# A decode kernel's last stage: FFN down projection and output projection in two column tiles, finer weight pieces, two stores

## The chip, the cores and the metric

The kernel runs on one core of one Trainium2 chip. The metric is the device time of one execution in microseconds (us). A profile belongs to one execution; its "span" runs from the first to the last recorded instruction and is about 1.7 us shorter than the device time. The profile also records the clock granted to PE as a share of full speed; in these traces it is 1.00 or 0.50 ("half clock"). The unchanged kernel took 201.09 us (median of 3 executions, 200.91 to 204.61).

The engines are called PE (TensorE matmul), PEld (its weight load), DVE (VectorE), ACT (ScalarE) and SP (SyncE). SPq and ACTq are DMA issues by the sequencers of SP and ACT.

## The reference

Four decode tokens of width 512 go through grouped-query attention over a window of 4096 cached positions (32 query heads, 8 key/value heads of width 128) and, from the same `x`, through a gated ReLU FFN of width 1792. A scalar gate mixes the two. Cut to what matters here:

```python
g = sigmoid((x * gate_w).sum(-1, keepdims=True))          # [4, 1, 1]
o = softmax(q @ k.T * Dh**-0.5) @ v                       # q = x @ wq; 4096 keys
a = o.reshape(4, 1, 4096) @ wo                            # output projection, wo: [4096, 512]
h = relu(x @ W_gate) * (x @ W_up)                         # [4, 1, 1792]
b = h @ W_down                                            # down projection, W_down: [1792, 512]
return g * a + (1 - g) * b                                # [4, 1, 512]
```

Keys, values and weights are 81 MB of bf16, and each is read once. This stream of loads is nearly the whole time.

## The kernel before

SP issues all loads in one fixed order. The last are W_down ("wd") and wo in five pieces of 16, 8, 4, 2 and 2 of its 32 blocks (a block is 128 rows by 512 columns, 128 KB):

```python
WO_PIECES = ((0, 16), (16, 24), (24, 28), (28, 30), (30, 32))
# ... in the order of loads:
return o + [("wg",), ("wu",), ("v", NSET - 1), ("wd",)] + [("wo", p) for p in range(len(WO_PIECES))]
```

Down projection and output projection accumulate into the same four rows of one PSUM bank, `ACC`, one after the other. The down projection's result is scaled by `1 - g` into SBUF (`T2`) before the output projection may overwrite the bank, and `FIN` combines both:

```python
def FFN():
    for i in range(14):
        mm(banks[ACC][0:4, :], hT[:, 4 * i:4 * i + 4], Wd[:, 512 * i:512 * i + 512], i == 0, i == 13, ...)
def WO(p):
    lo, hi = WO_PIECES[p]
    w = [("WO", p), ("T2",)] + [("E", "OQ", s) for s in range(NSET)]     # the piece, T2, attention's result
    for i in range(lo, hi):
        mm(banks[ACC][0:4, :], oq[:, i, :], Wo[:, i, :], i == 0, i == 31, ...)
# VectorE
def T2():   # t2 = (1 - g) * ACC
    v.tensor_scalar(t2[:, :], banks[ACC][0:4, :], gg[:, 1:2], None, op0=ALU.mult)
def FIN():  # osum = g * ACC + t2
    v.scalar_tensor_tensor(osum[:, :], banks[ACC][0:4, :], gg[:, 0:1], t2[:, :], ALU.mult, ALU.add)
# SyncE, at the end of its queue
e.dma_start(out.rearrange("b o d -> (b o) d"), osum[0:4, :])
```

(Cuts: waits and events of FFN, T2 and FIN.)

## Time and profile before

| | before |
|---|---|
| time, median | 201.09 us |
| span of the profiled execution | 199.34 us |
| loads' share of the 16 DMA engines' span | 95.2% |
| last piece of wo has landed | 194.73 us |
| PE has finished the output projection | 196.88 us |

First, two lines of the page: the queue of loads (packets, MB, share of 16 engines' span), and the engines' shares of the chain that ended last (the work followed back from the last instruction, at each step to what it had waited for).

```profile
q1 hardware_dynamic: 3760, 81.01, 95.2%
DMA 73%; PE 21%; DVE 2%; SPq 2%; issue 0%
```

The loads take the DMA engines nearly the whole span. The chain's end, in order of time (start us, duration us, what):

```profile
149.34 40.41 DMA slots<-in_A_wo_dram
189.75 0.04 issue
189.80 7.08 PE bank L317 x32
196.88 0.02 issue
196.90 0.74 DVE osum L583
```

And the timeline of that stage (start us, duration us, engine, line, operation, tiles, count, and in brackets how long the engine was idle before and what ended that):

```profile
185.14 3.18 PE L317 MATMUL bank<-wdsb,hT 128*4 128x512 bf16 x14
188.36 0.74 DVE L579 TENSOR_SCALAR t<-bank,gg 4x512 f32<-4x512 f32 x1 [2.88 <-PE bank L317]
189.80 7.07 PE L317 MATMUL bank<-slots,oq 128*4 128x512 bf16 x32 [1.48 <-DMA slots<-in_A_wo_dram]
196.90 0.74 DVE L583 SCALAR_TENSOR_TENSOR osum<-bank,gg,t 4x512 bf16<-4x512 f32 x1 [7.81 <-PE bank L317]
197.67 0.29 SPq L276 DMA_DIRECT2D out_dram<-osum  x1
```

The projection begins when the first piece, half of wo, has landed. From there it runs without a pause at 221 ns per matmul. The trace also records when each of the 16 DMA engines reports its part of a transfer; the last report of the five pieces came at 189.75, 192.25, 193.46, 194.10 and 194.73. So PE finished 2.15 us after the last weight had landed, and at the very end the kernel is limited by PE, not by DMA.

### The profile page before, as it was taken

Reading aid. Unit: us, or ns where it says so; the run is one execution under the profiler, and the core shown is the slowest. Engines: PE = TensorE matmul, PEld = TensorE weight load, DVE = VectorE, ACT = ScalarE, POOL = GpSimd, SP = SyncE. Lnnn points to the kernel's source line nnn. Section 1 sums busy time; section 2 is a strip of 40 time slices with the busy share of each in tenths; the row PEclk is TensorE's granted clock in tenths of the full one; section 3 lists DMA queues with packets and bytes.
Section 4 is the critical chain, followed back from the end, with each engine's and each line's share of the span. In section 5 each row is a group of like instructions: output and inputs, shape, how many; then the busy total and the mean of one; then the engine's idle time right before and its main releaser. Section 6 shows DMA issues by size and latency. Waiting matters only on the chain.

```text
span 199.3 us, 4082 instructions
## 1 busy us (share of the span) xinstructions
PE 145.7 (73%) x1806; PEld 110.9 (56%) x1806; DVE 104.7 (53%) x244; ACT 67.6 (34%) x70; POOL 13.2 (7%) x38
## 2 busy tenths in 40 slices
PE   0039865997199839974998599639974997577795
PEld 0039522875197639754976587439754975434231
DVE  2017566886068637862596388607862786310201
ACT  2006522751435343524353455134524451410000
POOL 7774000000000000000000000000000000000000
PEclk9999999999579996997699789988998799576999
DMA  5999999999999999999999999999999999999960
GB/s 210 434 415 427 429 444 434 454 419 427 418 427 434 437 427 431 421 441 437 427 427 424 436 424 421 431 422 434 450 434 418 415 411 448 432 408 424 401 253 1
DMA packets 3778, 81.28 MB, mean 408 GB/s; under 512 B 552, under 2 KB 560, under 8 KB 944
## 3 DMA queue, kind: packets, MB, share of 16 engines
q1 hardware_dynamic: 3760, 81.01, 95.2%
q8 instruction: 14, 0.23, 0.5%
q14 instruction: 4, 0.03, 0.0%
HBM read 81.01 MB, written 0.00 MB: 406 GB/s over the span
## 4 chain that ended last, share of the span: by engine, by line
DMA 73%; PE 21%; DVE 2%; SPq 2%; issue 0%
DMA slots<-in_A_k_cache_dram 43%; DMA slots<-in_A_wo_dram 20%; DMA slots<-in_A_wq_dram 11%; PE bank L321 10%; PE bank L317 10%; SPq L250 2%; DVE qblk L525 1%; DVE osum L583 0%; DVE sc L535 0%; DVE pe L510 0%; DVE pe L512 0%; DVE gp L515 0%
## 5 line engine op out<-in xcount | busy, mean ns | idle before, releaser
L321 PE MATMUL bank<-identf,slots 128*128 128x128 f32 x512 | 73.2, 304 | 31.4 <-DMA slots<-in_A_k_cache_dram 31.4
L321 PEld LDWEIGHTS bank<-identf,slots 128*128 128x128 f32 x512 | 65.5, 159 | 39.3 <-DMA slots<-in_A_k_cache_dram 32.1
L503 DVE COPY slots<-bank 128x1024 bf16<-128x1024 bf16 x80 | 54.3, 690 | 51.0 <-PE bank L321 49.4
L596 ACT ACTIVATE slots<-bank 128x1024 bf16<-128x1024 bf16 x48 | 47.8, 1022 | 63.6 <-PE bank L321 63.4
L618 ACT ACTIVATE pe<-sc,negmax 128x2048 bf16<-128x2048 bf16 x8 | 16.0, 2001 | 37.9 <-DVE negmax L547 37.9
L535 DVE TENSOR_SCALAR_CACHE_REDUCE sc<-bank 128x512 bf16<-128x512 f32 x32 | 22.1, 692 | 3.6 <-PE bank L317 1.2
L317 PE MATMUL bank<-slots,qblk 128*32 128x512 bf16 x256 | 20.5, 394 | 1.3 <-DVE qblk L525 1.2
L317 PE MATMUL bank<-slots,pT 128*32 128x256 bf16 x512 | 17.0, 290 | 1.7 <-DMA slots<-in_A_v_cache_dram 1.7
L317 PEld LDWEIGHTS bank<-slots,pT 128*32 128x32 bf16 x512 | 14.5, 102 | 4.2 <-DMA slots<-in_A_v_cache_dram 1.7
L321 PE MATMUL bank<-identb,pe 128*128 128x128 bf16 x128 | 11.6, 261 | 2.2 <-ACT pe L618 2.2
L553 DVE COPY pT<-bank 128x1024 bf16<-128x1024 bf16 x16 | 10.6, 686 | 3.9 <-PE bank L321 3.8
L317 PE MATMUL bank<-maskr,maskl 128*32 128x512 bf16 x128 | 12.5, 378 | 0.0
L321 PEld LDWEIGHTS bank<-identb,pe 128*128 128x128 bf16 x128 | 10.8, 123 | 2.8 <-ACT pe L618 2.3
L561 DVE TENSOR_SCALAR osb<-bank,recip 128x256 bf16<-128x256 f32 x8 | 3.9, 483 | 12.9 <-PE bank L317 12.9
L317 PE MATMUL bank<-rd,grpb 128*128 128x8 bf16 x8 | 1.4, 179 | 10.1 <-DVE rd L541 10.1
L317 PEld LDWEIGHTS bank<-rd,grpb 128*128 128x128 bf16 x8 | 0.8, 95 | 14.1 <-DVE rd L541 14.1
L317 PE MATMUL bank<-slots,oq 128*4 128x512 bf16 x32 | 7.1, 379 | 1.5 <-DMA slots<-in_A_wo_dram 1.5
L317 PEld LDWEIGHTS bank<-slots,qblk 128*32 128x32 bf16 x256 | 4.6, 95 | 6.1 <-issue 3.5
L317 PEld LDWEIGHTS bank<-slots,oq 128*4 128x4 bf16 x32 | 2.6, 85 | 5.9 <-DMA slots<-in_A_wo_dram 2.0
L317 PEld LDWEIGHTS bank<-maskr,maskl 128*32 128x32 bf16 x128 | 3.4, 95 | 3.9
L317 PE MATMUL bank<-slots,xT 128*4 128x512 bf16 (+1 forms) x64 | 5.1, 476 | 0.3 <-DMA slots<-in_A_wq_dram 0.3
L583 DVE SCALAR_TENSOR_TENSOR osum<-bank,gg,t 4x512 bf16<-4x512 f32 x1 | 0.7, 739 | 7.8 <-PE bank L317 7.8
(57 smaller groups left out, 58.9 us busy)
## 6 DMA issues: line engine op xcount, KB each, us to landing
slots<-in_A_k_cache_dram SPq DMA_DIRECT2D x8, 4096.0 KB, 42.7
slots<-in_A_v_cache_dram SPq DMA_DIRECT2D x8, 4096.0 KB, 33.5
slots<-in_A_wq_dram SPq DMA_DIRECT2D x1, 4096.0 KB, 21.1
slots<-in_A_wo_dram SPq DMA_DIRECT2D x1, 2048.0 KB, 40.4
slots<-in_B_W_gate_dram SPq DMA_DIRECT2D x1, 1792.0 KB, 38.5
slots<-in_B_W_up_dram SPq DMA_DIRECT2D x1, 1792.0 KB, 42.1
wdsb<-in_B_W_down_dram SPq DMA_DIRECT2D x1, 1792.0 KB, 36.1
slots<-in_A_wo_dram SPq DMA_DIRECT2D x1, 1024.0 KB, 42.4
```

Source lines behind the costliest of these rows:

```text
L250: E.op(lambda: e.dma_start(dst, src), ev=ev, waits=waits, ctr=ctr)
L317: E.op(lambda: t.matmul(out_, lhsT, rhs, start=start, stop=stop, tile_position=pos, skip_group_check=True), ev=ev, waits=waits)
L321: E.op(lambda: t.transpose(out_, in_, idn), ev=ev, waits=waits)
L503: E.op(lambda: v.tensor_copy(kt_dst(s, g), bankb[tr(key)]), ev=("E",) + key, waits=[key])
L525: E.op(lambda dst=dst, r=r, b=b: v.tensor_copy(dst, src[r, :, :, :, b]), ev=("E",) + key if (u, b) == (1, 3) else None, waits=[key, ("QZ",)])
L535: E.op(lambda: v.tensor_scalar(sc[:, 512 * f:512 * f + 512], banks[scb(key)], 1.0, None, op0=ALU.mult, op1=ALU.max, accum_out=mx4[:, f:f + ...
L553: E.op(lambda: v.tensor_copy(dst, bankb[tr(key)]), ev=("E",) + key, waits=[key] + ([("PV", s - 2)] if s >= 2 else []))
L561: E.op(lambda: v.tensor_scalar(osb[:, s % 2, :], ob(s), recip[:, s % 2:s % 2 + 1], None, op0=ALU.mult), ev=("NORM", s), waits=[("E", "RS", ...
L583: E.op(lambda: v.scalar_tensor_tensor(osum[:, :], banks[ACC][0:4, :], gg[:, 0:1], t2[:, :], ALU.mult, ALU.add), ev=("OSUM",), waits=[("WOP ...
L596: E.op(lambda: a.activation(kt_dst(s, g), bankb[tr(key)], ACTF.Copy), ev=("E",) + key, waits=[key])
L618: E.op(lambda: a.activation(pe[:, :], sc[:, :], ACTF.Exp, bias=negmax[:, s % 2:s % 2 + 1], scale=SCALE, accum_out=rowsum[:, s % 2:s % 2 + ...
```

## The change

The intent is to have less to do after the last weight has landed. The two projections write 256 columns each to PSUM rows 0 to 3 and 64 to 67, by matmuls at array columns 0 and 64. T2 and FIN then work on 128 rows by 256 columns (only eight rows carry results; the bank is cleared at the start, so that the others hold defined values). The result lies on two groups of rows and needs two stores, one from SP and one from ACT. The first piece of wo is halved, and a 64-byte load, "again", is put last in the queue. The diff's core:

```diff
-WO_PIECES = ((0, 16), (16, 24), (24, 28), (28, 30), (30, 32))
+WO_PIECES = ((0, 8), (8, 16), (16, 24), (24, 28), (28, 30), (30, 32))
+OUTT = 2
+OW = 512 // OUTT
+OR = 128 // OUTT
@@ order of loads
-    ... + [("wo", p) for p in range(len(WO_PIECES))]
+    ... + [("wo", p) for p in range(len(WO_PIECES))] + [("again",)]
@@ FFN (WO and the gate's Z likewise)
-                mm(banks[ACC][0:4, :], hT[:, 4 * i:4 * i + 4], Wd[:, 512 * i:512 * i + 512], i == 0, i == 13, ...)
+                for j in range(OUTT):
+                    x = 512 * i + OW * j
+                    mm(banks[ACC][OR * j:OR * j + 4, 0:OW], hT[:, 4 * i:4 * i + 4], Wd[:, x:x + OW], i == 0, i == 13,
+                       ..., pos=(0, OR * j))
@@ FIN (T2 likewise)
-            v.scalar_tensor_tensor(osum[:, :], banks[ACC][0:4, :], gg[:, 0:1], t2[:, :], ALU.mult, ALU.add)
+            v.scalar_tensor_tensor(osum[:, :], banks[ACC][:, 0:OW], gg[:, 0:1], t2[:, :], ALU.mult, ALU.add)
@@ stores: t = 0 from SP, t = 1 from ACT
-        e.dma_start(out.rearrange("b o d -> (b o) d"), osum[0:4, :])
+        e.dma_start(out.rearrange("b o d -> (b o) d")[:, OW * t:OW * t + OW], osum[OR * t:OR * t + 4, :])
```

More of the change, by code (lines that the diff above doesn't have):

```diff
@@ L109, in _alloc @@
     sb("gwT", [128, 4], BF16)
+    sb("again", [8, 4], BF16)
     sb("osb", [128, 2, 256], BF16)
@@ L127, in _alloc @@
     sb("recip", [128, 2], FP32)
-    sb("ge", [4, 2], FP32)
-    sb("gp", [4, 2], FP32)
-    sb("gg", [4, 2], FP32)
-    sb("t2", [4, 512], FP32)
-    sb("osum", [4, 512], BF16)
+    sb("ge", [128, 2], FP32)
+    sb("gp", [128, 2], FP32)
+    sb("gg", [128, 2], FP32)
+    sb("t2", [128, OW], FP32)
+    sb("osum", [128, OW], BF16)
     R["banks"] = [ctx.enter_context(nc.psum_tensor(f"bank{i}", [128, 512], FP32)) for i in range(8)]
@@ L154, in _dma_order @@
         o += [("k", s), ("v", s - 1)]
-    return o + [("wg",), ("wu",), ("v", NSET - 1), ("wd",)] + [("wo", p) for p in range(len(WO_PIECES))]
+    return o + [("wg",), ("wu",), ("v", NSET - 1), ("wd",)] + [("wo", p) for p in range(len(WO_PIECES))] + [("again",)]
 def _slots():
@@ L164, in _slots @@
         k = it[0]
-        if k in ("x", "gw", "wd") or (k == "wo" and it[1] > 0):
+        if k in ("x", "gw", "wd", "again") or (k == "wo" and it[1] > 0):
             continue
@@ L244, in ob, with store @@
         return banks[OB][:, 256 * (s % 2):256 * (s % 2) + 256]
+    def store(E, e, t):
+        E.op(lambda: e.dma_start(out.rearrange("b o d -> (b o) d")[:, OW * t:OW * t + OW], osum[OR * t:OR * t + 4, :]),
+             ev=("OUT", t), waits=[("OSUM",)], ctr=f"d_out{t}")
     def sync(e):
@@ L258, in sync @@
                 load(("GW",), "d_gw", gwT[:, :], gate_w.rearrange("(p t) -> p t", t=4))
+            elif k == "again":
+                load(("AGAIN",), "d_again", R["again"][0:8, :], gate_w[0:32].rearrange("(p t) -> p t", t=4))
             elif k == "wq":
@@ L275, in sync @@
                      waits=w)
-        E.op(lambda: e.dma_start(out.rearrange("b o d -> (b o) d"), osum[0:4, :]), ev=("OUT",), waits=[("OSUM",)],
-             ctr="d_out")
-        E.wait([("OUT",)])
+        for t in range(0, OUTT, 2):
+            store(E, e, t)
+        E.wait([("OUT", t) for t in range(OUTT)] + [("AGAIN",)])
     def gpsimd(e):
@@ L340, in Z @@
             for q in range(4):
-                mm(banks[ACC][0:4, 0:1], xT[:, 4 * q:4 * q + 4], gwT[:, q:q + 1], q == 0, q == 3,
-                   ev=("Z",) if q == 3 else None, waits=[("E", "XT"), ("GW",)])
+                for j in range(OUTT):
+                    mm(banks[ACC][OR * j:OR * j + 4, 0:1], xT[:, 4 * q:4 * q + 4], gwT[:, q:q + 1], q == 0, q == 3,
+                       ev=("Z",) if (q, j) == (3, OUTT - 1) else None, waits=[("E", "XT"), ("GW",), ("INIT",)],
+                       pos=(0, OR * j))
         def Q():
@@ L436, in FFN @@
             for i in range(14):
-                mm(banks[ACC][0:4, :], hT[:, 4 * i:4 * i + 4], Wd[:, 512 * i:512 * i + 512], i == 0, i == 13,
-                   ev=("FFN",) if i == 13 else None, waits=[("E", "HT"), ("WD",), ("GE",)])
+                for j in range(OUTT):
+                    x = 512 * i + OW * j
+                    mm(banks[ACC][OR * j:OR * j + 4, 0:OW], hT[:, 4 * i:4 * i + 4], Wd[:, x:x + OW], i == 0, i == 13,
+                       ev=("FFN",) if (i, j) == (13, OUTT - 1) else None, waits=[("E", "HT"), ("WD",), ("GE",)],
+                       pos=(0, OR * j))
         def WO(p):
@@ L443, in WO @@
             for i in range(lo, hi):
-                mm(banks[ACC][0:4, :], oq[:, i, :], Wo[:, i, :], i == 0, i == 31, ev=("WOP", p) if i == hi - 1 else None,
-                   waits=w if i == lo else ())
+                for j in range(OUTT):
+                    mm(banks[ACC][OR * j:OR * j + 4, 0:OW], oq[:, i, :], Wo[:, i, OW * j:OW * j + OW], i == 0, i == 31,
+                       ev=("WOP", p) if (i, j) == (hi - 1, OUTT - 1) else None, waits=w if (i, j) == (lo, 0) else (),
+                       pos=(0, OR * j))
         fns = dict(KT=KT, XT=XT, Z=Z, Q=Q, QT=QT, SC=SC, PT=PT, PV=PV, SW=SW, RS=RS, OQ=OQ, WO=WO, GU=GU, HT=HT, FFN=FFN)
@@ L497, in INIT @@
             E.op(lambda: v.memset(qblk[:, :, :, :], 0.0), ev=("QZ",))
-            for bk in SCB:
-                E.op(lambda bk=bk: v.memset(banks[bk], 0.0), ev=("INIT",) if bk == SCB[-1] else None)
+            for bk in SCB + (ACC,):
+                E.op(lambda bk=bk: v.memset(banks[bk], 0.0), ev=("INIT",) if bk == ACC else None)
         def EKT(s, g):
@@ L578, in T2 @@
         def T2():
-            E.op(lambda: v.tensor_scalar(t2[:, :], banks[ACC][0:4, :], gg[:, 1:2], None, op0=ALU.mult), ev=("T2",),
+            E.op(lambda: v.tensor_scalar(t2[:, :], banks[ACC][:, 0:OW], gg[:, 1:2], None, op0=ALU.mult), ev=("T2",),
                  waits=[("FFN",), ("G",)])
         def FIN():
-            E.op(lambda: v.scalar_tensor_tensor(osum[:, :], banks[ACC][0:4, :], gg[:, 0:1], t2[:, :], ALU.mult, ALU.add),
+            E.op(lambda: v.scalar_tensor_tensor(osum[:, :], banks[ACC][:, 0:OW], gg[:, 0:1], t2[:, :], ALU.mult, ALU.add),
                  ev=("OSUM",), waits=[("WOP", len(WO_PIECES) - 1), ("T2",), ("G",)])
@@ L606, in GE @@
             for u in range(2):
-                E.op(lambda u=u: a.activation(ge[:, u:u + 1], banks[ACC][0:4, 0:1], ACTF.Exp, scale=-1.0 if u == 0 else 1.0),
+                E.op(lambda u=u: a.activation(ge[:, u:u + 1], banks[ACC][:, 0:1], ACTF.Exp, scale=-1.0 if u == 0 else 1.0),
                      ev=("GE",) if u else None, waits=[("Z",)])
@@ L623, in scalar @@
             fns[it[0]](*it[1:])
+        for t in range(1, OUTT, 2):
+            store(E, a, t)
     return [("tensor", tensor), ("vector", vector), ("scalar", scalar), ("gpsimd", gpsimd), ("sync", sync)]
```

## The prediction

> **What bounds the kernel now.** The load queue. The page gives it 95.2% of the 16 DMA engines' span, 81 MB; the chain of waits is 73% DMA. Only its end is not DMA: the chain in order of time closes with the wo load until 189.75, 32 output-projection matmuls for 7.08 us (221 ns each), the final vector operation for 0.74 us (to 197.64), and the store, issued at 197.67, which lands at 198.94; the span ends at 199.34. The trace's landing records show the five wo pieces complete at 189.75, 192.25, 193.46, 194.10 and 194.73. The projection starts late, because its first piece is half of wo, and runs at PE's pace: the last piece lies in SBUF 2.15 us before PE finishes.
>
> **What the change does.**
> 1. Each 512-column matmul becomes two of 256 at array columns 0 and 64. [...]64 attention-value matmuls of 256 columns in four tiles took 1.92 us (30 ns each, timeline at 165.23). I expect about 110 ns per pair: the projection's work 3.6 us in place of 7.1, FFN 1.7 in place of 3.2.
> 2. The first wo piece is halved. By the queue's rate 1 MB takes 2.4 us, so wo's first quarter lands near 187.3, just as FFN (from 185.1) and its scaling end. PE then waits for each piece and works it off before the next lands.
> 3. After the last landing at 194.73 only four matmuls are left: about 0.43 us at full clock.[...]
> 4. The final vector operation works on 128x256 in place of 4x512. The 128x256 scaling from PSUM takes 483 ns, the 4x512 one 739: -0.26 us.
> 5. Two 2 KB stores from two queues: no bytes saved, the same issue-to-landing time (1.27 us now). The Scalar queue's first transfer may add 0 to 0.4 us.
> 6. The tiny load behind the last wo piece: no gain; the last piece's landing came 0.43 us after its last data, the one before 0.45 us though followed by another.
> 7. Off the path: 50 more matmuls, one 0.49 us bank clear, smaller descriptors in 1 MB[...].
>
> **Sum.** 194.75 + 0.45 to 0.65 + 0.5 + 1.7 to 1.9 = span 197.4 to 197.8, against 199.34: -1.5 to -1.9 us. Of the 5 us that PE and vector save, only what lies behind the last landing counts; the load stream stays.
>
> **Prediction.** 199.4 us, range 198.7 to 200.4. Faster by over 2%: 0.02; within 2%: 0.96; slower by over 2%: 0.02.
>
> **What would show it.** Right: last wo landing at 194.4 to 195.3, PE waiting on DMA before every wo piece, projection ending at most 0.8 us after the last landing, final vector operation near 0.48 us, from its end to the span's end 1.6 to 2.1 us. Wrong: projection still over 5 us behind its first landing, Scalar store landing much later than Sync's, last landing moved.
>
> **What would make it wrong.** The slow DMA engines set the last landing: per-engine completions of the last piece spread from 191.25 to 194.73. If the instruction fetches (14, 1.1 us each on one engine) fall differently, the end moves by up to about 1 us. A slow first Scalar store would eat the gain.

The sum came to a span of 197.4 to 197.8 us. The 110 ns per pair of matmuls is an estimate; it is half of the 221 ns that one 512-column matmul took. The 0 to 0.4 us for the Scalar queue's first transfer was an allowance; an issue of 0.62 us in place of 0.28 was measured later.

## The result

The changed kernel took 199.74 us (median of 4, 199.68 to 199.85), against 201.19 us (median of 4) for the kernel before beside it. The ratio of the times is 0.993 (95% interval 0.991 to 0.995): a small gain, within 2%. Ratios here are the mean time of one kernel's fast runs over that of the other's of the same rounds, so not quite the ratio of the quoted medians.

After the change, in the views shown of the kernel before: the page's lines for the loads and for the chain's engines, then the end of the chain, then the timeline.

```profile
q1 hardware_dynamic: 3920, 81.01, 95.9%
DMA 65%; PE 23%; SPq 7%; DVE 3%; issue 1%
```

```profile
162.45 32.77 DMA slots<-in_A_wo_dram
195.22 0.04 issue
195.27 0.40 PE bank L327 x4
195.67 0.02 issue
195.69 0.48 DVE osum L600
```

```profile
185.41 3.15 PE L327 MATMUL bank<-wdsb,hT 128*4 128x256 bf16 x28
188.60 0.48 DVE L596 TENSOR_SCALAR t<-bank,gg 128x256 f32<-128x256 f32 x1 [2.85 <-PE bank L327]
189.23 2.08 PE L327 MATMUL bank<-slots,oq 128*4 128x256 bf16 x32 [0.67 <-DVE t L596]
...
192.73 1.04 PE L327 MATMUL bank<-slots,oq 128*4 128x256 bf16 x16 [1.43 <-DMA slots<-in_A_wo_dram]
...
194.00 1.02 PE L327 MATMUL bank<-slots,oq 128*4 128x256 bf16 x12 [0.23 <-DMA slots<-in_A_wo_dram]
...
195.27 0.38 PE L327 MATMUL bank<-slots,oq 128*4 128x256 bf16 x4 [0.24 <-DMA slots<-in_A_wo_dram]
195.69 0.48 DVE L600 SCALAR_TENSOR_TENSOR osum<-bank,gg,t 128x256 bf16<-128x256 f32 x1 [6.61 <-PE bank L327]
196.20 0.28 SPq L251 DMA_DIRECT2D out_dram<-osum  x1
196.21 0.62 ACTq L251 DMA_DIRECT2D out_dram<-osum  x1
```

The loads' share went up a little, to 95.9%, for the same bytes in a shorter span. The chain's shares moved mainly because it is followed back through the issue of loads by SP for a while; nothing here rests on that. The chain's last matmul piece is 4 matmuls in place of 32, and it begins when the last of wo lands. From the 8 blocks of the third piece on (192.73), the timeline shows PE waiting for DMA before each piece; the second piece, in the same line as the first, landed at 190.22 and was begun at 190.26. The span fell by 1.33 us, from 199.34 to 198.01. Step by step:

| step | before, us | after, us |
|---|---|---|
| last landing of wo | 194.73 | 195.22 |
| from there to the projection's end | 2.15 | 0.45 |
| FIN | 0.74 | 0.48 |
| FIN's end to the span's end | 1.70 | 1.84 |

Two things need an explanation. The last landing came 0.49 us later. And the down projection, which should have taken half as long in two tiles, took 3.15 us, as before.

### The profile page after: what moved, and what is told of

The parts are those of the page before. It is cut to its first block, busy times and chain, and to the rows that moved or that the text cites. A ratio compares the mean times of both kernels' runs of the same rounds, so it can differ in the third digit from the quotient of the medians.

```text
span 198.0 us, 4187 instructions
## 1 busy us (share of the span) xinstructions
PE 147.5 (74%) x1856; PEld 116.4 (59%) x1856; DVE 105.3 (53%) x245; ACT 67.4 (34%) x70; POOL 13.2 (7%) x38
## 3 DMA queue, kind: packets, MB, share of 16 engines
q1 hardware_dynamic: 3920, 81.01, 95.9%
## 4 chain that ended last, share of the span: by engine, by line
DMA 65%; PE 23%; SPq 7%; DVE 3%; issue 1%
DMA slots<-in_A_k_cache_dram 49%; DMA slots<-in_A_wo_dram 17%; PE bank L331 16%; SPq L258 7%; PE bank L327 7%; DVE qblk L542 1%; DVE sc L552 0%; DVE pe L527 0%; DVE slots L520 0%; DVE osum L600 0%; DVE pe L529 0%; DVE xT L523 0%
## 5 line engine op out<-in xcount | busy, mean ns | idle before, releaser
L331 PE MATMUL bank<-identf,slots 128*128 128x128 f32 x512 | 75.5, 311 | 28.5 <-DMA slots<-in_A_k_cache_dram 28.5
L331 PEld LDWEIGHTS bank<-identf,slots 128*128 128x128 f32 x512 | 68.3, 164 | 35.7 <-DMA slots<-in_A_k_cache_dram 29.2
L331 PE MATMUL bank<-identb,pe 128*128 128x128 bf16 x128 | 13.7, 291 | 2.2 <-ACT pe L635 2.2
L331 PEld LDWEIGHTS bank<-identb,pe 128*128 128x128 bf16 x128 | 12.9, 139 | 2.7 <-ACT pe L635 2.3
L327 PE MATMUL bank<-slots,oq 128*4 128x256 bf16 x64 | 4.5, 272 | 2.6 <-DMA slots<-in_A_wo_dram 1.9
L327 PE MATMUL bank<-osb,fold 128*64 128x32 bf16 x64 | 3.6, 189 | 0.7 <-DVE osb L578 0.7
```

Source lines behind the costliest of these rows:

```text
L327: E.op(lambda: t.matmul(out_, lhsT, rhs, start=start, stop=stop, tile_position=pos, skip_group_check=True), ev=ev, waits=waits)
L331: E.op(lambda: t.transpose(out_, in_, idn), ev=ev, waits=waits)
```

## The experiments

There were eleven runs, eight of them of edited kernels, in three groups on two chips. Those of one group share their runs of the kernel before; the second and third group, on one chip, also share eleven of these between them. The diffs are cut to the lines that matter: shapes of tiles, waits and events are left out. My theory was that the tiles are the whole gain, because only the work behind the last landing counts, and that the other parts do nothing. Rivals: the finer pieces are needed too; the tiny load or the smaller transfers moved the last landing; smaller matmuls, rather than two column groups at once, made the gain.

### The tiles alone

```diff
-WO_PIECES = ((0, 8), (8, 16), (16, 24), (24, 28), (28, 30), (30, 32))
+WO_PIECES = ((0, 16), (16, 24), (24, 28), (28, 30), (30, 32))
-    ... + [("again",)]
```

> The two column tiles and two stores alone, with the five old wo pieces and without the tiny load. Theory (the tiles are the whole gain; what counts is the work left behind the last landing): the first 32 matmuls start at the landing of half of wo near 189.8, are done near 191.7, before the next landing near 192.3, so the coarse first piece costs nothing: 199.6 to 199.8 us, as the whole change. Rival (the finer pieces are needed): PE is still behind at the last landing, 200.2 us or more.

Measured: 199.64 us (199.47 to 199.68, 6 runs), ratio 0.990 (0.986 to 0.993), so the whole gain. In its profile the clock stood at half until 193.44, and still (timeline):

```profile
190.12 5.37 PE L327 MATMUL bank<-slots,oq 128*4 128x256 bf16 x64 [1.22 <-DMA slots<-in_A_wo_dram]
195.53 0.48 DVE L600 SCALAR_TENSOR_TENSOR osum<-bank,gg,t 128x256 bf16<-128x256 f32 x1 [6.11 <-PE bank L327]
```

The last piece landed at 195.06, and PE was done 0.43 us later. The first 32 matmuls were not done near 191.7, as I had expected: at half clock they ended at 193.85, 1.3 us after the second piece had landed (192.55). At full clock PE then caught up just in time, about 0.1 us before the last landing. The finer pieces added nothing to the tiles in these runs; with a longer half clock they might have.

### The pieces and the tiny load alone

Here the new `WO_PIECES` and "again" went into the kernel before, with its 512-column matmuls and one store.

> The kernel before with the finer wo pieces and the tiny load, without column tiles. Theory: the projection stays at PE's pace (7.08 us for 32 matmuls) but can start when the FFN's scaling ends, near 189.1, in place of 189.80: it ends near 196.2 and the time falls by about 0.6 to 0.7 us, to about 200.5. Rival (pieces do nothing without tiles): 201.1 to 201.2.

Measured: 200.40 to 202.93 us, median 201.34, ratio 1.000 (0.995 to 1.005). Three of six runs were near 200.6, three at 201.8 and above; the next section but one shows what slows the kernel before in that way; the slow runs here were not traced. The profiled one is of the first kind (timeline):

```profile
188.45 0.74 DVE L582 TENSOR_SCALAR t<-bank,gg 4x512 f32<-4x512 f32 x1 [2.88 <-PE bank L320]
189.33 7.07 PE L320 MATMUL bank<-slots,oq 128*4 128x512 bf16 x32 [0.92 <-DVE t L582]
196.44 0.74 DVE L586 SCALAR_TENSOR_TENSOR osum<-bank,gg,t 4x512 bf16<-4x512 f32 x1 [7.25 <-PE bank L320]
```

What ended PE's wait is now T2 and no longer a load. The projection starts 0.47 us earlier than in the first trace of the kernel before, and all of it ends 0.46 us earlier. That is somewhat less than the 0.6 to 0.7 us expected, and not a gain to be seen in the mean of all runs.

### Without the tiny load

```diff
-    ... + [("wo", p) for p in range(len(WO_PIECES))] + [("again",)]
+    ... + [("wo", p) for p in range(len(WO_PIECES))]
```

> The changed kernel without the tiny load last in the queue. Theory (it does nothing): 199.65 to 199.8 us, last wo landing still near 195.2. Rival 1 (it delays the last landing, which came at 195.22 in place of 194.73): last landing near 194.8 and 0.3 to 0.5 us faster. Rival 2 (it speeds the last landing up): slower by 0.2 us or more.

Measured: 199.48 us (199.13 to 199.92), ratio 0.989 (0.986 to 0.992); the last landing came at 195.17. The tiny load does nothing that these runs can see. By chance this profile had full clock in the down projection (1.00 from 185.20 to 188.20; timeline):

```profile
185.30 1.70 PE L327 MATMUL bank<-wdsb,hT 128*4 128x256 bf16 x28
187.04 0.48 DVE L596 TENSOR_SCALAR t<-bank,gg 128x256 f32<-128x256 f32 x1 [1.40 <-PE bank L327]
187.75 1.04 PE L327 MATMUL bank<-slots,oq 128*4 128x256 bf16 x16 [0.75 <-DMA slots<-in_A_wo_dram]
```

So the two tiles halve the down projection, from 3.18 to 1.70 us, and PE waits even for the first piece. Its FIN began at 195.64, that of the changed kernel's first profile, with 3.15 us for the down projection, at 195.69. Between these two traces, a down projection twice as fast was worth nothing at the end.

### The kernel before, traced twice more

> The kernel before, unchanged, traced again: how far its last wo landing (194.73 in its one trace) and the clock of its last stage differ from execution to execution. If the later last landing of the changed kernel (195.22) is only scatter between executions, this one lies anywhere in 194.7 to 195.3; if the change itself moved it, it stays within 0.1 us of 194.73.[...]

> As before_2: a third trace of the kernel before. Last wo landing in 194.7 to 195.3 if scatter, within 0.1 us of 194.73 if the change had moved it; a slow execution (202 us or more) should show half clock in the projection.

Measured: 202.32 and 202.05 us, last landings 195.16 and 194.93. The timeline of the first of them:

```profile
185.28 4.85 PE L317 MATMUL bank<-wdsb,hT 128*4 128x512 bf16 x14 [0.20 <-DMA wdsb<-in_B_W_down_dram]
...
190.17 0.74 DVE L579 TENSOR_SCALAR t<-bank,gg 4x512 f32<-4x512 f32 x1 [4.83 <-PE bank L317]
...
191.06 7.07 PE L317 MATMUL bank<-slots,oq 128*4 128x512 bf16 x32 [0.92 <-DVE t L579]
198.16 0.74 DVE L583 SCALAR_TENSOR_TENSOR osum<-bank,gg,t 4x512 bf16<-4x512 f32 x1 [7.25 <-PE bank L317]
```

And what the clock was in the down projection. Each line is a stretch, its length, the busy time of PE, PEld, DVE, ACT and POOL with the number of instructions, the granted clock, the DMA share and GB/s. First the first trace of the kernel before, then this one, then the changed kernel.

```profile
185.20:188.20 3.00, 3.00 (x15) 1.04 (x14) 0.23 (x1) 0.00 (x0) 0.00 (x0) 1.00 1.00 414
```

```profile
185.20:188.20 3.00, 2.92 (x7) 0.85 (x8) 0.15 (x1) 0.00 (x0) 0.00 (x0) 0.50 0.97 404
```

```profile
185.20:188.20 3.00, 3.00 (x34) 1.86 (x32) 0.23 (x1) 0.00 (x0) 0.00 (x0) 0.50 0.98 401
```

This answers both open points.

1. *The last landing scatters.* In three traces of the kernel before it came at 194.73, 194.93 and 195.16. In the traces of the two unedited runs of the changed kernel it came at 195.22 and 195.33, in the other experiments shown with the same rows per load between 195.00 and 195.17. The first trace of the kernel before happened to be the earliest of all twelve. Whether the change itself costs 0.1 or 0.2 us here stays open; 0.49 us it does not.
2. *The down projection runs at half clock in some executions of either kernel.* In the kernel before this lies on the critical path: the down projection takes 4.85 us, T2 ends at 190.91, and the projection starts at 191.06, held up by T2 and not by its weights. The time goes up by 1.26 us (span 200.60 in place of 199.34). In the changed kernel T2 ended at 189.08 at half clock, and PE had caught up with the loads at the second piece, begun at 190.26.

I had expected the half clock in the projection itself; it was in the stage before it. In the first traces of the kernel before and of the changed kernel the stretches of equal clock last 3.41 us or whole multiples of it, and they lie elsewhere in each: the last one at half clock within the span went from 180.49 to 183.90 in the one and from 172.16 to 189.22 in the other. In the three traces of the kernel before the clock in the down projection (185.20 to 188.20) was 1.00 once and 0.50 twice. So the same kernel has several speeds. Twelve runs of the kernel before on this chip: the five with a mean clock of 0.897 or more took 201.12 to 201.47 us; the other seven, 0.864 to 0.890, took 201.40 to 203.53. For single runs this is a correlation; the two traces show the mechanism, for times up to 202.32 us. What made three runs slower still (202.87 to 203.53) was not traced. The changed kernel's six runs beside them took 199.34 to 200.32 us with clocks of 0.871 to 0.904 in no such order.

### Two column groups, or only smaller matmuls?

From the kernel with finer pieces and no tiles, with each matmul cut into two halves at the same array columns and output rows:

```diff
-                mm(banks[ACC][0:4, :], oq[:, i, :], Wo[:, i, :], i == 0, i == 31, ...)
+                for j in range(2):
+                    mm(banks[ACC][0:4, 256 * j:256 * j + 256], oq[:, i, :], Wo[:, i, 256 * j:256 * j + 256], i == 0, i == 31, ...)
```

> The kernel before with the finer pieces and the tiny load (as b_pieces_alone), and each 512-column matmul cut into two halves of 256, but both halves at the same array columns and output rows 0 to 3, one store. Theory (the gain is two column groups at work at once, not smaller matmuls): the projection's 64 matmuls take 7.0 to 7.4 us at full clock, the end as in b_pieces_alone, 200.4 to 201.9 us. Rival (smaller matmuls or less to do after the last landing suffice): under 200 us.

Measured: 200.61 us (200.47 to 202.81), ratio 0.995 (0.990 to 1.001). The result is wrong (relative error 0.12), which I had not foreseen. The instructions and their times are still what was to be measured (timeline):

```profile
185.12 3.22 PE L320 MATMUL bank<-wdsb,hT 128*4 128x256 bf16 x28
...
189.26 7.15 PE L320 MATMUL bank<-slots,oq 128*4 128x256 bf16 x64 [0.93 <-DVE t L585]
```

28 matmuls take 3.22 us, against 1.70 us for the same 28 in two column groups, both at full clock (1.00), and the 64 of the projection take 7.15 us. Splitting alone gains nothing; the two column groups at work at once are the gain. What makes the result wrong, no run here shows. In the change the halves lie in different rows of the bank (0 to 3 and 64 to 67), and its results are correct.

### The first transfer of the Scalar queue

The ACT store's issue took 0.62 us, that of SP 0.28. In this experiment ACT issues "again" as its very first instruction, and SP does not:

```diff
-    ... + [("again",)]
@@ scalar program, first of all
+        E.op(lambda: a.dma_start(R["again"][0:8, :], gate_w[0:32].rearrange("(p t) -> p t", t=4)), ev=("AGAIN",), ctr="d_again")
```

> The changed kernel with its tiny load issued first of all from the Scalar queue in place of last from the Sync queue, so that the Scalar queue's store is not that queue's first transfer. Theory (the Scalar store's 0.62 us issue, against 0.28 us on Sync, is a cost of first use): issue near 0.3 us, both stores land together 1.2 us after issue, from the end of the final vector operation to the span's end 1.70 us in place of 1.84, 0.1 to 0.2 us faster. Rival (the Scalar queue always issues that slowly): 0.62 us again and the same time.

Measured (timeline):

```profile
196.10 0.29 SPq L251 DMA_DIRECT2D out_dram<-osum  x1
196.10 0.28 ACTq L251 DMA_DIRECT2D out_dram<-osum  x1
```

The issue fell to 0.28 us, and that of the 64-byte load, now the first on this queue, took 0.58 us. So the 0.62 us were a cost of first use. But nothing came of it: the later of the two stores still landed 1.35 us after its issue, as in the changed kernel (then ACT's, 196.21 to 197.56; now SP's, 196.10 to 197.45, with ACT's at 197.28). From FIN's end to the span's end it was 1.79 us, against 1.84. The time was 199.92 us, ratio 0.990 (0.985 to 0.994), no faster than the changed kernel on the same chip in the next group (199.67). No run here issued both stores from one queue, so what two queues gain over one was not shown; the two 2 KB stores took 1.35 us from issue to landing, the single 4 KB store 1.27 us.

### Which DMA engines are late

The last piece's 16 completions in the changed kernel spread from 191.31 to 195.22, with six of them after 194.5. The eight completions of "again" ended at 193.58, each 0.18 to 0.21 us after one of the last piece's, so by this match none of its engines was one of the late six. The next kernel puts 15 tiny loads, of 1 to 15 rows, last in the queue:

```diff
-    ... + [("again",)]
+    ... + [("again", k) for k in range(1, 16)]
-                load(("AGAIN",), "d_again", R["again"][0:8, :], gate_w[0:32].rearrange("(p t) -> p t", t=4))
+                load(("AGAIN", it[1]), f"d_again{it[1]}", R["again"][0:it[1], 4 * it[1]:4 * it[1] + 4],
+                     gate_w[0:4 * it[1]].rearrange("(p t) -> p t", t=4))
```

> A measurement, not a faster kernel: 15 tiny loads of 1 to 15 rows last in the Sync queue in place of one of 8. In the changed kernel the tiny load's 8 completions all belong to DMA engines that finish early (to 193.58), none to the six that finish at 194.6 to 195.2. If a load of k rows runs on the first k engines, its completions show which engine is late: expected are some of engines 9 to 16, and the last wo landing near 195.2.

Measured: a load of k rows reported k completions (beside one immediate report), and each larger one added one engine to those of the smaller. The engines are numbered here in that order: engine 0 is the one that the load of one row used, engine 15 the one that none of them reached; the trace itself names no engine. The time at which each engine reported its part of wo's last piece, put together from these reports, in us:

```
engine  0       1       2       3       4       5, 6            7       8
        191.58  192.24  192.12  193.43  191.63  193.13, 193.18  191.78  191.73
engine  9       10      11      12      13      14      15
        194.62  194.71  194.75  194.64  194.70  195.01  192.02
```

The late six are engines 9 to 14. The mean of the sixteen is 193.20, so by this estimate an evenly spread load would end 1.8 us earlier.

The traces also show how engines fall behind. Set in order of time, the sixteen reports of one load of 128 rows lie one common step after those of the load before (9.7 us for 4 MB), within 0.13 us, except for single reports that jump (the kernel with narrow loads, below, loses this step at its end). In all thirteen traces, from 23 us on, there are as many jumps of 1.1 to 2.0 us as instruction fetches of 16 KB before the end of the loads: 14, and 13 in the kernel with one mask matmul (below). In the changed kernel's first trace each of the 14 jumps (1.2 to 1.6 us) also falls into the stretch of one of the fetches (0.95 to 1.10 us each). In the map's trace two such jumps make up the 3.0 to 3.4 us by which engines 9 to 14 trail engine 0, and one the 1.6 us of engines 5 and 6. So the late engines fit a delay by two fetches each, and not a lower speed. This is a match in time: the trace does not name the engine of a fetch. Nor is the set fixed: in the control with halves in one column group, two of the eight completions of "again" came at 194.47 and 194.80.

### An attempt to use this

The last three of wo's 32 blocks come as DMAs of 63, 63 and 2 rows, meant to run on at most nine engines:

```diff
+WO_PIECES = ((0, 8), (8, 16), (16, 24), (24, 27), (27, 29), (29, 31), (31, 32))
+NARROW = (5, 6)
+ROWS = ((0, 63), (63, 126), (126, 128))
-                load(("WO", it[1]), f"d_wo{it[1]}", Wo[:, lo:hi, :], ...)
+                for n, (a, z) in enumerate(ROWS if it[1] in NARROW else ((0, 128),)):
+                    load(("WO", it[1], n), f"d_wo{it[1]}_{n}", Wo[a:z, lo:hi, :], ...)
```

> The changed kernel without the tiny load, with the last three of wo's 32 blocks (29 to 31) loaded as DMAs of 63, 63 and 2 rows, which should run on the first nine engines only (f_map: engines 10 to 15, counted from one, finish last, by 1.2 us or more), so that the late six carry 48 KB less... worked out per engine 24 KB less, 0.98 us. Theory (the lateness of those engines sets the end): the last landing of blocks 0 to 28 near 194.0, the rest by 194.3, projection's end 194.8 in place of 195.5, 0.4 to 0.7 us faster than the changed kernel of the same rounds. Rival (the lateness is not tied to those engines or the odd row counts cost more): same or slower.

Measured: 200.61 us (200.29 to 201.24), against 199.67 for the changed kernel beside the same runs: slower. The loads of 63 rows did report nine completions each. (The expectation's 0.98 us for 24 KB is an estimate; the mean of 408 GB/s on the page of the kernel before, over 16 engines, gives 0.96 us.) But the late six did not end earlier. Their part of blocks 0 to 28 landed at 195.15 in place of the 194.0 expected. From the second to the third piece (8 blocks) they needed 3.2 us, against 2.5 us in the changed kernel, while the other engines were already at the last pieces and the narrow loads. So the narrow loads slowed the others down; through what, was not tested. The end then also met a half clock (timeline):

```profile
193.08 1.04 PE L330 MATMUL bank<-slots,oq 128*4 128x256 bf16 x16 [2.20 <-DMA slots<-in_A_wo_dram]
...
194.45 1.97 PE L330 MATMUL bank<-slots,oq 128*4 128x256 bf16 x16 [0.33 <-DMA slots<-in_A_wo_dram]
```

The second 16 matmuls include a wait for the last landing at 195.34, and the clock was 0.50 from 194.66 on. A half clock at the end is the case from which the upper end of the forecast's sum came; none of the traces of the changed kernel shows it.

The comparison in these rounds was the changed kernel again:

> The changed kernel again, in the same rounds as the next two for a direct comparison: 199.5 to 200.0 us, last wo landing 194.9 to 195.3, time from last landing to the projection's end 0.4 to 0.5 us whatever the clock in the FFN.

Measured: 199.67 us (199.34 to 200.32), ratio 0.988 (0.984 to 0.993), last landing 195.33, the projection's end 0.45 us behind it, at a half clock in the down projection (3.15 us). As expected, but for single runs on either side of the range and a last landing 0.03 us beyond it.

### One instruction fetch less

In the changed kernel's trace the last of the six late engines fell behind only during the wo load. A 16 KB instruction fetch at 185.43 took 1.09 us on some engine. Set side by side in order of time (the trace does not name the engines), 15 of the 16 completions moved by about 2.5 us from wd's load to wo's first piece, and one by about 4 us (183.74 to 187.72); that one was then the last in every piece by 0.4 us. To be rid of that fetch, this kernel has one mask matmul over 128 columns in place of four over 32 for each score bank:

```diff
-            for e in range(3): ...   # e == 2: four matmuls with maskl [128, 32] at columns 32 * c
+            for e in range(2): ...
+            mm(bk[:, :], R["maskl"][:, :], R["maskr"][:, :], False, True, ev=key)      # maskl [128, 128]
```

> The changed kernel with one mask matmul over all 128 columns in place of four per score bank: 96 matmuls and as many weight loads fewer, so the last 16 KB instruction fetch (at 185.4, during the wo load) falls away or comes after the loads. Theory (that fetch holds one DMA engine up by 1.5 us and makes it the last): 13 fetches before 190 in place of 14, last wo landing near 194.8 in place of 195.2, 0.3 to 0.5 us faster than the changed kernel. Rival (smaller descriptors or the tiny load moved the last landing): last landing stays near 195.2, same time.

Measured: 199.61 us (198.96 to 199.79), ratio 0.989 (0.986 to 0.992), last landing 195.02, so not the gain expected. The last fetch moved to 193.62, but the one before it moved from 177.34 to 183.98 and now fell into the same stretch: again one engine came 0.3 us behind the other late ones. One fetch fewer fell before the end of the loads, and five engines were late in place of six. But the other four of them still landed at 194.65 to 194.74, so that even without the fetch at 183.98 the end would come, by this estimate, only some 0.3 us earlier. That a fetch holds an engine up fits; that this one alone set the end does not.

### What is left open

I found no version that beats the changed kernel. The tiles alone, the change without the tiny load, and the change with one mask matmul came out at 0.989 to 0.990 of the kernel before on one chip, with intervals that overlap. What the narrow loads collide with is open. The late engines fit the instruction fetches, but no run took away enough of them to bring the last landing forward.

## Why the prediction was right or wrong

The prediction was 199.4 us (198.7 to 200.4), and 199.74 was measured.

- **What bounds the kernel: right, with a gap.** The load stream stays, and only the end is PE's. What one trace could not tell is that the time of the kernel before depends on the clock in its down projection: at half clock the projection starts at 191.06 in place of 189.80. In the first comparison the change gained 0.7%, against before-runs of 200.91 to 201.28 (a fourth, 204.61, counts as slow and is left out); in the later groups, whose before-runs went up to 203.5, about 1.1%.
- **Pairs of matmuls at about 110 ns: right.** At full clock the down projection took 1.70 us, as predicted; the control without column groups took 3.22 us. In the first profile of the changed kernel it took 3.15 us, for the clock was half (0.50). That term was mis-sized by a factor of two there, and it cost nothing.
- **PE waits before every piece: right at full clock** (the run without the tiny load shows it from 187.75 on), **wrong in the first profile**, where the first piece had landed at 187.72 and PE waited for T2 until 189.08. It was right again from the second piece on (landed 190.22, begun 190.26).
- **Four matmuls behind the last landing, 0.43 us at full clock: right.** From landing to the projection's end it was 0.45 us.
- **FIN at 0.5 us: right,** 0.48.
- **Stores, FIN's end to the span's end 1.7 to 1.9 us: right,** 1.84. The first Scalar transfer was slower to issue, as feared (0.62 us against 0.28). That does not explain all of the 0.14 us over the single store (1.70): with an issue of 0.28 us it was still 1.79.
- **The tiny load gains nothing: right,** 199.48 us without it.
- **The last landing at 194.75: the one mis-sized term of the sum.** It was 195.22. The reading behind it, 194.73, was taken from one trace as if it were a constant, and was the earliest of twelve. It scatters from 194.73 to 195.16 in the kernel before alone. The prediction did name a moved landing as a risk. This term (+0.47 us) is the reason why the span of 198.01 us lay beyond the sum's own range (197.4 to 197.8), and more than the gap of 0.34 us between 199.4 and 199.74. The wide range of the time (198.7 to 200.4) allowed for it.

Measured term by term: 195.22 + 0.45 + 0.02 + 0.48 + 1.84 = 198.01 us of span.

## What to carry to other kernels

When loads fill the time, look at what is left to do behind the last landing. Of the matmul and vector time saved here (some 5 us at full clock) only 1.33 us of the span came back, and finer pieces without faster matmuls gave nothing certain. Trace the kernel before more than once: one trace had the fastest clock pattern and the earliest last landing, and a part whose speed follows the clock (the down projection: 3.18 us at 1.00, 4.85 us with most of it at 0.50) can sit on the critical path in one execution and not in the next. Matmuls of few rows whose results can lie in different rows of the bank (here 0 to 3 and 64 to 67) should be put in different column groups: here it halved their time (the down projection 1.70 us in place of 3.18 at full clock), and in the traces of the changed kernel a half clock in the down projection no longer moved the end. Count instruction fetches as part of the load: here the 14 of them, 0.95 to 1.10 us each, fit which engines landed last.
